# VectorE's complex products in fewer, longer operations: a third plane with minus the imaginary part, and products over both parts at once

## The chip, the cores and the metric

The kernel runs on one core of one Trainium2 chip. The metric is the device time of one execution in microseconds (us). The engines are named as in the profile: PE is TensorE, DVE is VectorE, ACT is ScalarE, POOL is GpSimd, SP is SyncE, which issues most of the DMAs. Each engine works through its own queue in order; they wait for each other at semaphores.

## What is computed

A linear attention with a complex decay, then a mixture of four experts over its output:

```python
B, H, S, D = 4, 8, 768, 48
a_n = a * min(|a|, 0.999) / (|a| + 1e-6)        # complex, a = a_re + i a_im
for t in range(S):                              # state S_t: complex, D x D for each batch and head
    state = a_n[t][:, None] * state + outer(k[t], v[t])
    y[t]  = q[t] @ real(state)
x = y as [B*S, H*D]                             # 3072 x 384
out = sum over e of p[:, e] * (relu(x @ w1[e]) @ w2[e])     # 4 experts, F = 1024, p normalised over e
```

All is float32.

## The kernel before

**Groups and chunks.** The 3072 rows are cut into 12 groups of 256 steps (g), three for each batch, and a group into two chunks of 128. A tile with q, k or a of a group has 128 partitions (head and feature) and 8 x 96 columns for each part: 8 steps in a row (SEG, index i) times 96 segments (MS: 3 blocks of heads by 32).

**From a to Q and K, on VectorE and ScalarE.** `load_a` (L355) brings the real and the imaginary part of a into a tile A of two buffers. `norm` (L399) finds the factor and multiplies A by it in place (L438). `prefix` (L441) turns A into running products: for i = 1 to 7 one product of all four combinations (L446), a subtract (L448) and an add (L449); then over the segments of a chunk with doubling width (`sk`, through `cmul`, L383: products L387 and L388, subtract L394, add L395); then the fill of all other steps (`fm`, products L390 to L393 one part at a time, then L394 and L395). `finish` (L483) has a head (L508), which finds the squared magnitude with a reduction that keeps the least value for a check at the end (L513, into `st_a2`), and multiplies q by A (L520), and a tail (L531), which divides k by A (L535 to L543). `rotate` (L685) multiplies the state by the product of a whole group: two products across the halves (L694, L695), one in place (L696), a sum (L697).

**What sets the order.** For group 0 all this stands alone at the start (`front(0, ...)`, L888): TensorE only splits the first weights, runs dummy matmuls (`turn_over`, L217) and does the small products of the near attention. From there `moe1(g - 1)` runs the experts 0 and 1 of one group on TensorE (`ph` L246 and `po` L267, each with float32 split in a high and a low part: `xh`/`xl`, `hh`/`hl`), and `between` (L942) weaves the front and the attention of the next groups in, by costs written out by hand (the numbers behind `yield`, STEP and MORE). In 4 steps of `moe1` an expert is done; its copies go to `acc` (L775) and by a POOL DMA to memory. The order on each engine is then fixed by a planner that goes by modelled lengths. The groups 0 and 1 use the near form, in two halves for the two chunks; the later ones do both chunks at once. At about 580 us the second stage begins (`c2`, L971): experts 2 and 3 in a form with fewer products (L995), in tiles that take the place of the first stage's.

Of the kernel before, what the change touches and what calls it, by code (L numbers as in the profile page):

```python
# [8 lines left out]
F32 = mybir.dt.float32  # L9
# [22 lines left out]
NA = 2  # L32
# [21 lines left out]
PRE = ("acc", "xh", "xl")  # L54
# [71 lines left out]
def fast_path(ctx, tc, qkP, aP, vP, probsP, w, out, flag):  # L126
# [54 lines left out]
    def stage1(i, tags):  # L181
        return stage_w(i, 1, moe.tile([P, 2 * HD], F32, tag=tags[i % len(tags)], name=f"wst{i}",
                                        bufs=1 if tags[i % len(tags)] == "x" else None))[:, 0]
# [114 lines left out]
    with ExitStack() as c1:  # L298
# [19 lines left out]
        nc.scalar.activation(maskp, m_ps[:, :2], AF.Copy)  # L318
# [8 lines left out]
        st_a2 = big.tile([P, CG, NG], F32, name="st_a2")  # L327
# [11 lines left out]
        nc.gpsimd.memset(TA, 0.0)  # L339
        band = moe.tile([P, HOFF + P + IM + C], F32, tag="x", name="band", bufs=1)  # L340
# [3 lines left out]
        nc.scalar.activation(near_mask, m_ps[:, 2], AF.Copy)  # L344
# [28 lines left out]
        def cmul(x, br, bi, shape, nm):  # L373
# [24 lines left out]

        def norm(g, A, parts=((0, SEG),), prev=(None, None, None)):  # L399
            s = tmp(f"s{g}")  # L400
            u = tmp(f"u{g}")
            for n, (lo, hi) in enumerate(parts):
# [35 lines left out]
                nc.vector.tensor_tensor(Af, Af, bc2(y0), op=ALU.mult)  # L438
                yield 1.75

        def prefix(g, A, cuts=(1, NS)):  # L441
            for i in range(1, SEG):
# [40 lines left out]
        def finish(g, A, qk):  # L483
# [24 lines left out]
            def head(lo, hi):  # L508
                nc.scalar.activation(some(a2a, lo, hi), some(A[:, 0], lo, hi), AF.Square)
                nc.scalar.activation(some(b2a, lo, hi), some(A[:, 1], lo, hi), AF.Square)  # L510
                for c in range(lo, hi):
                    a2, ic = some(a2a, c, c + 1), some(i0a, c, c + 1)
                    red = nc.vector.tensor_tensor_reduce(a2, a2, some(b2a, c, c + 1), scale=1.0, scalar=3e38,  # L513
                                                         op0=ALU.add, op1=ALU.min, accum_out=st_a2[:, c, g:g + 1])
# [4 lines left out]
                for c in range(2):  # L519
                    ins = nc.vector.tensor_tensor(dst(Q[:, c, :, :C], lo, hi), rows(A[:, c], lo, hi),  # L520
                                                  rows(qk[:, 0], lo, hi), op=ALU.mult)
                    if g < NSEL and lo == 1:
                        behind(ins, red)
                        last["qp"] = ins
# [6 lines left out]
            def tail(lo, hi):  # L531
# [5 lines left out]
                nc.vector.tensor_tensor(t, kn, t, op=ALU.mult)  # L537
                for c in range(2):
                    to, x, y = dst(K[0][:, c], lo, hi), rows(A[:, c], lo, hi), rows(ta, lo, hi)
                    if hi - lo == CG:  # L540
                        to = K[0][:, c].rearrange("p n (f i s) -> p (n f) i s", f=2, i=SEG)
                        x, y = (z.rearrange("p i (n s) -> p n i s", s=CS // 2) for z in (A[:, c], ta))
                    last_dve = nc.vector.tensor_tensor(to, x, y, op=ALU.mult)  # L543
# [15 lines left out]
        def t_factors(g):  # L559
# [5 lines left out]
            tc.keep_in_program_order(nc.scalar.activation(TB[IM:M], Ti, AF.Copy))  # L565
            tc.keep_in_program_order(nc.scalar.activation(TB[0:D], Ti, AF.Copy, scale=-1.0))
# [118 lines left out]
        def rotate(g):  # L685
# [96 lines left out]
        def check_all():  # L782
            nc.vector.tensor_scalar(st_m2, st_m2, M2_MIN, None, op0=ALU.is_ge)
            for c in range(CG):
                nc.vector.tensor_scalar(st_a2[:, c], st_a2[:, c], A2_MIN[c], None, op0=ALU.is_ge)
            nc.vector.tensor_scalar(st_w, st_w, W_MAX, None, op0=ALU.is_le)
            for c in range(CG):
                nc.vector.tensor_tensor(st_m2[:, :NG], st_m2[:, :NG], st_a2[:, c], op=ALU.mult)
# [10 lines left out]

# [744 lines left out]
```

## Time and profile before

| | |
|---|---|
| median of 3 runs | 961.46 us (960.48 to 963.05) |
| the profiled execution | 960.0 us, its span 958.2 us |
| granted TensorE clock | 0.999 of full speed |
| busy: PE, DVE, ACT, POOL | 933.9, 745.2, 483.0, 210.7 us |
| instructions: PE, DVE, ACT, POOL | 7388, 1630, 1030, 294 |
| chain that ended last | PE 89%, DVE 6%, DMA 3%, ACT 2% |

The span goes from the first to the last instruction; the rest of the execution's time lies around it. A row of the timeline gives the start, the length, engine, line, operation, output and inputs with their shapes; brackets at its end give the idle time before it and what ended that. In the table of stretches each engine has its busy time and the number of its instructions. A row of waits gives who waited for whom, the total in us, how often, and the longest.

### The profile page before, as it was taken

What the parts mean: (1) busy time and instruction counts of PE and PEld (TensorE: products, weight loads), DVE (VectorE), ACT (ScalarE), POOL (GpSimd) and SP (SyncE); (2) the same over time, 40 slices, a digit from 0 to 9 for tenths busy, and PEclk for the clock granted to TensorE, in tenths of its full rate; (3) what the DMA queues carried; (4) which work ended last, traced back from release to release, by engine and by line L of the source; (5) the groups of instructions that cost most, each with busy time, mean ns of one, the idle gap of its engine ahead of it and who ended that gap; (6) DMA issues with size and microseconds to landing.
All of it is one profiled execution on the core that took longest, in us unless ns stands there. A gap on an engine that the chain in (4) does not pass through costs nothing.

```text
span 958.2 us, 19409 instructions
## 1 busy us (share of the span) xinstructions
PE 933.9 (97%) x7388; PEld 908.3 (95%) x7388; DVE 745.2 (78%) x1630; ACT 483.0 (50%) x1030; POOL 210.7 (22%) x294
## 2 busy tenths in 40 slices
PE   5999999999999999999999999999999999999997
PEld 3899999999999999999999999999999999999997
DVE  7898989989989999888996577748485757666642
ACT  7766446363564736547343555635454554444430
POOL 6030111020211202111111036333424352322000
PEclk9999999999999999999999999999999999999999
DMA  9585264544535546353437799131514433131112
GB/s 314 171 172 139 60 159 89 150 99 142 149 96 129 129 138 156 117 135 109 117 109 226 269 316 275 50 121 38 148 57 144 162 85 102 50 99 51 50 50 78
DMA packets 75029, 125.73 MB, mean 131 GB/s; under 512 B 9600, under 2 KB 50224, under 8 KB 74928
## 3 DMA queue, kind: packets, MB, share of 16 engines
q1 hardware_dynamic: 60464, 94.69, 32.7%
q0 software_dynamic: 14464, 29.72, 13.3%
q8 instruction: 60, 0.98, 0.5%
q14 instruction: 41, 0.34, 0.1%
HBM read 75.94 MB, written 31.46 MB: 112 GB/s over the span
## 4 chain that ended last, share of the span: by engine, by line
PE 89%; DVE 6%; DMA 3%; ACT 2%; issue 1%; SPq 0%; ACTq 0%; DVEq 0%
PE ph L246 21%; PE pob L995 20%; PE po L267 19%; PE pb L995 17%; PE sc L635 3%; PE yp L667 2%; PE dp L611 2%; PE yp L677 2%; PE ktp L584 1%; DMA RX<-w 1%; PE sc L652 1%; DMA shi<-late_d 1%; DVE pf L446 1%; PE xp L706 1%; DVE xl L1001 0%
## 5 line engine op out<-in xcount | busy, mean ns | idle before, releaser
L995 PE MATMUL pob<-shi,hid 128*128 128x384 f32 x528 | 148.5, 335 | 0.5 <-DVE hid L1004 0.5
L267 PE MATMUL po<-whi,hh 128*128 128x384 f32 x384 | 129.7, 338 | 0.0
L267 PE MATMUL po<-wlo,hh 128*128 128x384 f32 x384 | 128.9, 336 | 0.0
L257 ACT ACTIVATE hh<-ph 128x512 fp32r<-128x512 f32 x96 | 57.2, 596 | 121.8 <-PE ph L246 117.5
L1007 POOL TENSOR_TENSOR Z<-Z 128x384 f32<-128x384 f32 x84 | 89.9, 1104 | 114.6 <-DMA Z<-y_d 57.0
L246 PE MATMUL ph<-xha,whi 128*128 128x256 f32 x576 | 103.8, 287 | 1.3 <-ACT xha L233 1.3
L246 PE MATMUL ph<-xla,whi 128*128 128x256 f32 x576 | 101.0, 283 | 2.0 <-DVE xla L235 2.0
L246 PE MATMUL ph<-xha,wlo 128*128 128x256 f32 x576 | 102.0, 284 | 0.0
L995 PE MATMUL pb<-xh,shi 128*128 128x384 f32 x291 | 97.1, 335 | 1.0 <-DVE pb L1001 1.0
L995 PEld LDWEIGHTS pob<-shi,hid 128*128 128x128 f32 x528 | 96.4, 188 | 1.2 <-DVE hid L1004 1.1
L995 PE MATMUL pb<-xl,shi 128*128 128x384 f32 x288 | 96.2, 334 | 0.0
L995 PE MATMUL pb<-xh,slo 128*128 128x384 f32 x288 | 96.2, 334 | 0.0
L246 PEld LDWEIGHTS ph<-xha,whi 128*128 128x128 f32 x576 | 85.9, 190 | 5.3 <-issue 2.4
L258 DVE SCALAR_TENSOR_TENSOR hl<-ph,hh 128x512 fp32r<-128x512 f32 x96 | 65.9, 687 | 31.0 <-ACT hh L257 30.3
L995 PE MATMUL pob<-slo,hid 128*128 128x384 f32 x264 | 88.2, 334 | 0.0
L267 PE MATMUL po<-whi,hl 128*128 128x384 f32 x384 | 85.2, 338 | 0.5 <-DVE hl L258 0.5
L246 PEld LDWEIGHTS ph<-xla,whi 128*128 128x128 f32 x576 | 82.8, 191 | 2.7 <-DVE xla L235 2.4
L246 PEld LDWEIGHTS ph<-xha,wlo 128*128 128x128 f32 x576 | 82.8, 190 | 0.4
L998 ACT ACTIVATE SN<-pb 128x384 f32<-128x384 f32 x96 | 47.4, 494 | 66.7 <-PE pb L995 59.4
L1001 DVE TENSOR_TENSOR xl<-Z,xh 128x384 fp32r<-128x384 f32 x104 | 59.2, 598 | 21.7 <-ACT xh L998 16.3
L998 ACT ACTIVATE hid<-pb 128x384 fp32r<-128x384 f32 x76 | 37.3, 491 | 71.9 <-PE pb L995 71.5
L267 PEld LDWEIGHTS po<-whi,hh 128*128 128x128 f32 x384 | 72.4, 189 | 0.3 <-ACT acc L775 0.2
(238 smaller groups left out, 2119.4 us busy)
## 6 DMA issues: line engine op xcount, KB each, us to landing
qk<-qkP SPq DMA_DIRECT2D x24, 384.0 KB, 4.0
acc_d<-acc POOLq DMA_DIRECT2D x24, 384.0 KB, 5.3
ACC<-acc_d SPq DMA_DIRECT2D x48, 192.0 KB, 3.2
A<-aP SPq DMA_DIRECT2D x22, 384.0 KB, 6.1
v<-vP SPq DMA_DIRECT2D x24, 288.0 KB, 3.0
Z<-y_d SPq DMA_DIRECT2D x16, 384.0 KB, 4.8
Qst<-Q SPq DMA_DIRECT2D x40, 145.1 KB, 3.9
Kst<-K SPq DMA_DIRECT2D x40, 144.0 KB, 3.8
```

Source lines behind the costliest of these rows:

```text
L246: ins = nc.tensor.matmul(ph[:, u, :], wt[:, j * P:(j + 1) * P], xt[:, j, :], start=(n == 0), stop=(n == 3 * NJ - 1))
L257: wts["hh"] = nc.scalar.activation(hh, ph, AF.Relu)
L258: nc.vector.scalar_tensor_tensor(hl, ph, 0.0, hh, op0=ALU.max, op1=ALU.subtract)
L267: nc.tensor.matmul(po[t], part[0][:, u, t * P:(t + 1) * P], wts[i][n][:, HD:], start=(i % FE == 0 and part[0] is hh and n == 0), stop=(i % ...
L611: ins = nc.tensor.matmul(d_ps[o:o + n, h, :], KT[:, c, h, o:o + n], vc[:, h * D:(h + 1) * D], start=True, stop=True)
L635: ins = nc.tensor.matmul(to, k, q, start=True, stop=True)
L667: ins = nc.tensor.matmul(yo, vc[:, vo:vo + n], scs[2 * c + h // 4][:, h % 4, :], start=True, stop=first)
L677: ins = nc.tensor.matmul(yo, st[:, o:o + n], Qc[:, o // D, :], start=False, stop=True)
L995: return tc.keep_in_program_order(nc.tensor.matmul(*args, **kw))
L998: return pin(nc.scalar.activation(dst, src, fn, scale=scale))
L1001: pin(nc.vector.tensor_tensor(dst, x, y, op=op))
L1007: nc.gpsimd.tensor_tensor(dst, x, y, op=op)
```

## The change

The normalised a goes to a new tile N with three planes: minus the imaginary part, the real part, the imaginary part. VectorE writes planes 1 and 2 from A; ScalarE writes plane 0 as a negated copy of plane 2, in two pieces. With it a prefix step is one product and one sum over both parts in place of a product, a subtract and an add; the first step of the later groups keeps the old form. The first level of the scan has one product in place of two, the fill has two products over both parts in place of four, and for the groups from 2 on Q and K have one product each in place of two. The reduction of the head becomes a plain add; the value for the check is copied out by ScalarE. In `rotate` ScalarE copies the state's halves across, and one product over all partitions follows. A and N have one buffer each, where A had two, so that the load of the next a comes behind the normalisation; `acc` goes from two buffers to one, one staged weight goes to the tile `y`, and one hidden tile of the second stage to another pool. The masks' copies on ScalarE come behind the negation.

```diff
@@ PRE and stage1
-PRE = ("acc", "xh", "xl")
+PRE = ("acc", "xh", "xl", "y", "xh", "xl")
...
+        tag = tags[i % len(tags)]
+        pool = small if tag == "y" else moe
...
@@ constants of the first stage
-        nc.scalar.activation(maskp, m_ps[:, :2], AF.Copy)
-        st_a2 = big.tile([P, CG, NG], F32, name="st_a2")
+        st_a2 = big.tile([P, NG, NJ, CG], F32, name="st_a2")
...
+        nc.gpsimd.memset(TB, 0.0)
...
-        nc.scalar.activation(near_mask, m_ps[:, 2], AF.Copy)
@@ load_a
-            A = big.tile([P, 2, SEG, MS], F32, tag="A", name=f"A{g}", bufs=NA)
+            A = big.tile([P, 2, SEG, MS], F32, tag="A", name=f"A{g}", bufs=1)
@@ cmul
-            if len(shape) < 3:
-                nc.vector.tensor_tensor(v1, x, bc2(br), op=ALU.mult)
-                nc.vector.tensor_tensor(v2, x, bc2(bi), op=ALU.mult)
+            if shape[1:] == [1]:
+                z = tmp(f"{nm}z").rearrange("p c n -> p (c n)")[:, :4 * n].rearrange("p (c d n) -> p c d n", c=2, d=2)
+                v1, v2 = (z[:, k].unsqueeze(3) for k in range(2))
+                part, (col, _), _ = br.ap
+                nc.vector.tensor_tensor(z, x[:, :, :, 0].unsqueeze(1).broadcast_to([P, 2, 2, n]),
+                                        bass.AP(br.tensor, br.offset, [part, (SEG * MS, 2), (0, 2), (col, n)]), op=ALU.mult)
             else:
-                nc.vector.tensor_tensor(v1[:, 0], x[:, 0], br, op=ALU.mult)
-                nc.vector.tensor_tensor(v2[:, 1], x[:, 1], bi, op=ALU.mult)
-                nc.vector.tensor_tensor(v1[:, 1], x[:, 1], br, op=ALU.mult)
-                nc.vector.tensor_tensor(v2[:, 0], x[:, 0], bi, op=ALU.mult)
+                nc.vector.tensor_tensor(v1, x, both(br), op=ALU.mult)
+                nc.vector.tensor_tensor(v2, x, both(bi), op=ALU.mult)
@@ norm
+            N = planes[g] = big.tile([P, 3, SEG, MS], F32, tag="N", name=f"N{g}", bufs=1)
...
-                nc.vector.tensor_tensor(Af, Af, bc2(y0), op=ALU.mult)
+                last["an"] = nc.vector.tensor_tensor(N[:, 1:, lo:hi].rearrange("p c i m -> p c (i m)"), Af, bc2(y0),
+                                                     op=ALU.mult)
+                rows = (max(lo, 1), hi) if hi - lo < SEG else (2, 5, SEG)
+                for r0, r1 in zip(rows, rows[1:]):
+                    last["neg"] = nc.scalar.activation(N[:, 0, r0:r1], N[:, 2, r0:r1], AF.Copy, scale=-1.0)
@@ prefix
-                nc.vector.tensor_tensor(z, x.unsqueeze(2).broadcast_to([P, 2, 2, MS]), bc2(A[:, :, i - 1, :]),
-                                        op=ALU.mult)
-                nc.vector.tensor_tensor(x[:, 0], z[:, 0, 0], z[:, 1, 1], op=ALU.subtract)
-                nc.vector.tensor_tensor(x[:, 1], z[:, 1, 0], z[:, 0, 1], op=ALU.add)
+                if g > 0 and i == 1:
...
+                else:
+                    w, b = N[:, :2, i, :], N[:, 2, i - 1, :]
+                    part, plane, col = w.ap
+                    nc.vector.tensor_tensor(z, bass.AP(w.tensor, w.offset, [part, plane, plane, col]),
+                                            bass.AP(b.tensor, b.offset, [part, (-plane[0], 2), (0, 2), col]),
+                                            op=ALU.mult)
+                    nc.vector.tensor_tensor(x, z[:, 0], z[:, 1], op=ALU.add)
@@ finish, head and tail
+                red = nc.vector.tensor_tensor(some(a2a, lo, hi), some(a2a, lo, hi), some(b2a, lo, hi), op=ALU.add)
                 for c in range(lo, hi):
                     a2, ic = some(a2a, c, c + 1), some(i0a, c, c + 1)
-                    red = nc.vector.tensor_tensor_reduce(a2, a2, some(b2a, c, c + 1), scale=1.0, scalar=3e38,
-                                                         op0=ALU.add, op1=ALU.min, accum_out=st_a2[:, c, g:g + 1])
...
+                if hi - lo == CG:
+                    nc.vector.tensor_tensor(Q[:, :, :, :C].rearrange("p c n (i s) -> p i c n s", i=SEG),
...
+                ends = a2a.rearrange("p i (j n s) -> p j n i s", j=NJ, n=CG)[:, :, lo:hi, SEG - 1, CS - 1]
+                behind(nc.scalar.activation(st_a2[:, g, :, lo:hi], ends, AF.Copy), last_act)
...
@@ rotate (t_factors writes TB with the signs exchanged)
-            nc.vector.tensor_tensor(turned[0:D], Gt[IM:M], bt(TB[IM:M]), op=ALU.mult)
-            nc.vector.tensor_tensor(turned[IM:M], Gt[0:D], bt(TB[0:D]), op=ALU.mult)
+            nc.scalar.activation(turned[0:D], Gt[IM:M], AF.Copy)
+            nc.scalar.activation(turned[IM:M], Gt[0:D], AF.Copy)
             nc.vector.tensor_tensor(Gt, Gt, bt(TA), op=ALU.mult)
+            nc.vector.tensor_tensor(turned, turned, bt(TB), op=ALU.mult)
@@ moe1, late_weights, grab
-                acc = moe.tile([P, CG, HD], F32, tag="acc", name=f"acc{g}_{e}")
+                acc = moe.tile([P, CG, HD], F32, tag="acc", name=f"acc{g}_{e}", bufs=1)
-            raw = big.tile([P, 4, NJ, P], F32, tag="A", name=f"lw{i}", bufs=NA)
+            raw = big.tile([P, 4, NJ, P], F32, tag="AN"[len(late_raw) % 2], name=f"lw{i}", bufs=1)
-                    tag = {0: "x", 1: "xh", 2: "xl", 7: "xh", 8: "xl", 9: "acc", 10: "acc"}[k]
+                    tag = {0: "x", 1: "xh", 2: "xl", 7: "xh", 8: "xl", 9: "acc", 10: "hid"}[k]
...
@@ the start
-        A.append(load_a(1))
         for _ in norm(0, A[0], parts=halves):
             pass
+        A.append(load_a(1, prev=last["an"]))
         lin = last["lin"]
+        behind(nc.scalar.activation(maskp, m_ps[:, :2], AF.Copy), last["neg"])
+        behind(nc.scalar.activation(near_mask, m_ps[:, 2], AF.Copy), last["neg"])
...
-            lp = split_w(i, wst[i], ((ps_o, "po"), (ps_h, "ph")), prev=lin)
+            lp = split_w(i, wst[i], ((ps_o, "po"), (ps_h, "ph")), prev=lin if i < NPRE - 1 else last["neg"])
```

## Rows read from the trace of the kernel before

**Rows 1.** The page, part 1: busy time, share of the span, instructions.

```profile
PE 933.9 (97%) x7388; PEld 908.3 (95%) x7388; DVE 745.2 (78%) x1630; ACT 483.0 (50%) x1030; POOL 210.7 (22%) x294
```

**Rows 2.** Table of stretches: length, busy time by engine, clock, DMA share, GB/s.

```profile
25.00:50.00 25.00, 23.27 (x238) 20.52 (x237) 20.38 (x44) 18.15 (x40) 1.95 (x4) 1.00 0.51 158
...
150.00:200.00 50.00, 47.34 (x449) 45.03 (x449) 46.28 (x100) 26.24 (x55) 5.91 (x12) 1.00 0.42 108
200.00:500.00 300.00, 299.98 (x2952) 291.70 (x2951) 275.25 (x621) 153.93 (x326) 39.05 (x73) 1.00 0.49 128
...
550.00:610.00 60.00, 58.48 (x371) 57.15 (x370) 41.57 (x87) 35.10 (x77) 28.66 (x35) 1.00 0.87 246
...
950.00:958.20 8.20, 1.95 (x12) 1.63 (x10) 0.62 (x1) 0.00 (x0) 0.00 (x0) 0.94 0.11 32
```

**Rows 3.** Waits of TensorE, whole span: us in total, times, longest.

```profile
PE ph L246 <- DVE xla L235: 2.0, 1, 2.0
PE ph L246 <- ACT xha L233: 1.3, 2, 0.7
...
PE ktp L584 <- DVE K L543: 0.6, 1, 0.6
...
PE qp L478 <- DVE Q L520: 0.2, 1, 0.2
```

**Rows 4.** Timeline of VectorE at the start: start, length, line, operation.

```profile
15.72 0.56 DVE L446 TENSOR_TENSOR pf<-A 128x384 f32<-128x384 f32 x1
16.31 0.26 DVE L448 TENSOR_TENSOR A<-pf 128x96 f32<-128x96 f32 x1
16.49 0.25 DVE L449 TENSOR_TENSOR A<-pf 128x96 f32<-128x96 f32 x1
16.77 0.56 DVE L446 TENSOR_TENSOR pf<-A 128x384 f32<-128x384 f32 x1
...
20.00 0.26 DVE L387 TENSOR_TENSOR sk_1a<-A 128x96 f32<-128x96 f32 x1
...
20.47 0.21 DVE L394 TENSOR_TENSOR A<-sk_1a 128x48 f32<-128x48 f32 x1
...
23.18 0.48 DVE L390 TENSOR_TENSOR fm_1a<-A 128x315 f32<-128x315 f32 x1
...
24.89 0.48 DVE L394 TENSOR_TENSOR A<-fm_1a 128x315 f32<-128x315 f32 x1
```

**Rows 5.** Timeline at the stall near 150 us, VectorE and TensorE.

```profile
149.34 0.83 DVE L390 TENSOR_TENSOR fm_1a<-A 128x651 f32<-128x651 f32 x1
...
152.33 0.55 DVE L235 TENSOR_TENSOR xla<-xp,xha 128x384 fp32r<-128x384 f32 x1
...
152.93 0.62 PE L246 MATMUL ph<-xla,whi 128*128 128x256 f32 x3 [1.99 <-DVE xla L235]
```

**Rows 6.** Timeline behind the first normalisation, VectorE and ScalarE.

```profile
9.21 0.96 DVE L438 TENSOR_TENSOR A<-A,u 128x768 f32<-128x768 f32 x1
...
9.90 0.52 ACT L427 ACTIVATE u<-u 128x384 f32<-128x384 f32 x1
10.20 0.57 DVE L446 TENSOR_TENSOR pf<-A 128x384 f32<-128x384 f32 x1
...
14.50 0.60 ACT L435 ACTIVATE u<-u,neg 128x384 f32<-128x384 f32 x1
```

**Rows 7.** ScalarE's groups by line, up to 560 us: busy us, mean ns | idle before.

```profile
L588 ACT ACTIVATE KT<-ktp 128x288 f32<-128x288 f32 x40 | 16.7, 417 | 26.3 <-PE ktp L584 26.3
...
L619 ACT ACTIVATE Gs<-dp 112x384 f32<-112x384 f32 x4 | 2.0, 492 | 12.8 <-PE dp L611 12.8
```

**Rows 8.** Timeline: first reader of the second a, first matmul of the experts.

```profile
35.84 0.85 ACT L407 ACTIVATE s<-A 128x768 f32<-128x768 f32 x1
...
50.56 0.62 PE L246 MATMUL ph<-xha,whi 128*128 128x256 f32 x3 [0.58 <-ACT xha L233]
```

**Rows 9.** Waits of ScalarE from 60 to 550 us.

```profile
ACT hh L257 <- PE ph L246: 114.5, 53, 6.6
```

More of the change, by code (lines that the diff above doesn't have):

```diff
@@ L31 @@
 TMP = 4
-NA = 2
 NF1 = E1 * FE
@@ L181, in stage1 @@
     def stage1(i, tags):
-        return stage_w(i, 1, moe.tile([P, 2 * HD], F32, tag=tags[i % len(tags)], name=f"wst{i}",
-                                        bufs=1 if tags[i % len(tags)] == "x" else None))[:, 0]
+        tag = tags[i % len(tags)]
+        pool = small if tag == "y" else moe
+        return stage_w(i, 1, pool.tile([P, 2 * HD], F32, tag=tag, name=f"wst{i}",
+                                       bufs=1 if tag in ("x", "y", "acc") else None))[:, 0]
     def cast_w(i):
@@ L518, in head @@
                     last_act = nc.scalar.activation(ic, ic, AF.Exp, scale=-1.0, bias=a2e[:, c:c + 1])
[L519 to L524, printed above, removed]
+                if hi - lo == CG:
+                    nc.vector.tensor_tensor(Q[:, :, :, :C].rearrange("p c n (i s) -> p i c n s", i=SEG),
+                                            A.rearrange("p c i (n s) -> p i c n s", n=NR),
+                                            rows(qk[:, 0], lo, hi).unsqueeze(2).broadcast_to([P, SEG, 2, NR, CS]),
+                                            op=ALU.mult)
+                else:
+                    for c in range(2):
+                        ins = nc.vector.tensor_tensor(dst(Q[:, c, :, :C], lo, hi), rows(A[:, c], lo, hi),
+                                                      rows(qk[:, 0], lo, hi), op=ALU.mult)
+                        if lo == 1:
+                            behind(ins, red)
+                            last["qp"] = ins
+                ends = a2a.rearrange("p i (j n s) -> p j n i s", j=NJ, n=CG)[:, :, lo:hi, SEG - 1, CS - 1]
+                behind(nc.scalar.activation(st_a2[:, g, :, lo:hi], ends, AF.Copy), last_act)
                 if hi == CG:
@@ L784, in check_all @@
             for c in range(CG):
-                nc.vector.tensor_scalar(st_a2[:, c], st_a2[:, c], A2_MIN[c], None, op0=ALU.is_ge)
+                nc.vector.tensor_scalar(st_a2[:, :, :, c], st_a2[:, :, :, c], A2_MIN[c], None, op0=ALU.is_ge)
             nc.vector.tensor_scalar(st_w, st_w, W_MAX, None, op0=ALU.is_le)
             for c in range(CG):
-                nc.vector.tensor_tensor(st_m2[:, :NG], st_m2[:, :NG], st_a2[:, c], op=ALU.mult)
+                for j in range(NJ):
+                    nc.vector.tensor_tensor(st_m2[:, :NG], st_m2[:, :NG], st_a2[:, :, j, c], op=ALU.mult)
             nc.vector.tensor_tensor(st_m2, st_m2, st_w, op=ALU.mult)
@@ L830, in fast_path, with front @@
         qk = load_qk(0)
-        A.append(load_a(1))
         for _ in norm(0, A[0], parts=halves):
             pass
+        A.append(load_a(1, prev=last["an"]))
         lin = last["lin"]
+        behind(nc.scalar.activation(maskp, m_ps[:, :2], AF.Copy), last["neg"])
+        behind(nc.scalar.activation(near_mask, m_ps[:, 2], AF.Copy), last["neg"])
         cuts = (1, NS // CG, NS)
         todo = {}
-        def front(g, A, qk):
-            pre = prefix(g, A, cuts if g < NSEL else (1, NS))
-            Q, K, head, tail = finish(g, A, qk)
+        def front(g, qk):
+            pre = prefix(g, cuts if g < NSEL else (1, NS))
+            Q, K, head, tail = finish(g, planes[g][:, 1:], qk)
             def ahead():
@@ L885, in fast_path @@
         for i in range(NPRE):
-            lp = split_w(i, wst[i], ((ps_o, "po"), (ps_h, "ph")), prev=lin)
+            lp = split_w(i, wst[i], ((ps_o, "po"), (ps_h, "ph")), prev=lin if i < NPRE - 1 else last["neg"])
         turn_over(WARM[0], lp)
-        for _ in front(0, A[0], qk):
+        for _ in front(0, qk):
             pass
@@ L907, in stream @@
                     A.append(load_a(g + 1, prev=last["q"]))
-                for r in front(g, A[g], qk):
+                for r in front(g, qk):
                     yield g, r
@@ L1186, in grab @@
                 else:
-                    tag = {0: "x", 1: "xh", 2: "xl", 7: "xh", 8: "xl", 9: "acc", 10: "acc"}[k]
-                    t = moe.tile([P, 2 * TB2], F32R, tag=tag, name=f"hid{k}", bufs=1 if tag == "x" else None)
+                    tag = {0: "x", 1: "xh", 2: "xl", 7: "xh", 8: "xl", 9: "acc", 10: "hid"}[k]
+                    t = (fin if tag == "hid" else moe).tile([P, 2 * TB2], F32R, tag=tag, name=f"hid{k}",
+                                                            bufs=1 if tag in ("x", "acc", "hid") else None)
                 return t[:, :TB2], t[:, TB2:]
```

33 lines of the change are left out of this document (25 added, 8 removed).

## The prediction

> **What bounds the kernel now.** I read the engine shares first. TensorE is busy 97% of the span, VectorE 78%, ScalarE 50% [rows 1]. A change of VectorE's work can therefore only win back time in which TensorE stands still, and the share of 78% says nothing yet. The second view is the table of stretches [rows 2]; in it the reader is to compare TensorE's busy time with the length of each stretch. From 200 to 500 us it is busy 299.98 of 300 us although VectorE is busy 275.25 of them: there, less work on VectorE buys nothing. TensorE's idle time lies in four places: the start (25 to 50 us is 1.7 us idle, though much of its work there is dummy matmuls of `turn_over`, which hold nothing up), 2.7 us in 150 to 200, 1.5 us in 550 to 610, and 6.2 us behind 950, where the last rows are only written out. The third view, TensorE's waits [rows 3], says which of it is VectorE's: 2.0 us at one place for `xla` (L235), 0.6 us for K (L543), 0.2 us for Q (L520). The waits for `xha` (1.3 us) end on ScalarE and DMA, and VectorE has no part in them.
>
> So two places decide. **The start:** from the first normalised half to the first K, VectorE runs one chain of dependent operations: the prefix over 8 rows, the scan, the fill [rows 4]. **One stall at 150 us:** TensorE waits for the second `xla` piece of group 2, which stands in VectorE's queue behind four fill products, and starts 0.6 us after it [rows 5].
>
> **The price of a VectorE operation.** An operation of 96 elements lasts 0.25 us and the next one that does not need its result starts 0.18 us after it; one that needs it starts 0.28 us after it [rows 4]. One of 651 elements lasts 0.83 us, and four in a row take 2.99 us, 0.75 each [rows 5]. Hence 1.045 ns for an element (0.58 us over 555), some 0.15 us fixed in the duration, but only 0.07 us fixed between starts. From that, as estimates: 192 elements 0.35 us, 630 elements 0.81, 1302 elements 1.51. A merge of two independent operations saves 0.07 us, not 0.15.
>
> **The start, added up.** A prefix step now goes subtract, add, next product: 0.46 us from L448 to the next L446 [rows 4]. With one sum of 192 elements it is 0.35 + 0.03 = 0.38: 0.08 saved, in seven steps 0.56. The first scan level has two products in 0.47 us up to L394 [rows 4]; as one of 192 elements 0.38: 0.09 saved. The fill has four products in 1.71 us up to its subtract [rows 4]; as two of 630 elements 0.73 + 0.81 + 0.03 = 1.57: 0.14 saved, and the second fill of group 0 lies on the same chain: 0.28. The reduce of the head loses its accumulator read, but its result goes to ScalarE at the same moment: 0. Together 0.93 us.
>
> Against it stands a new hop. The prefix of group 0 needs the negated plane from its first step, so after the normalisation (L438 at 9.21, 0.96 long) ScalarE has to negate rows 1 to 3 before the first product, which now starts at 10.20 [rows 6]. ScalarE is in L427 until 10.42; the negation, 288 elements, costs 0.42 by the nearest row [rows 7]; so the product could start at 10.86, 0.66 late. If VectorE puts L428, which needs only L427, ahead of it, 0.28 us are lost instead. The second half's negation may stand behind L435 (14.50, 0.60 long and a read [rows 6]); that gives 0 to 0.4 us at step 4. The small copy of `st_a2` stands on ScalarE ahead of the K transposes' eviction: 0.1. The hop costs 0.3 to 1.1 us; I take 0.5, nearer the low end, because the other half's normalisation is there to fill it. Net gain 0.4 us; bounds 0.65 gained and 0.2 lost. TensorE sets a lid as well: in front of Q and K it only waits 0.2 + 0.6 us [rows 3], the rest is dummy matmuls in its queue, so no more than 0.8 us can be won before the first K.
>
> **The stall at 150 us.** Since VectorE's last idle moment before it (a wait for scores) its queue holds six pairs of subtract and add, the first scan level and the four fill products. 6 x 0.08 + 0.09 + (2.99 - 2 x 1.43 = 0.13) = 0.70 us. If the order stays, `xla` comes 0.7 us earlier and the stall falls from 2.0 to 1.3. But the program's order is computed anew from the changed lengths, and where `xla` lands among two longer products is open: between all 2.0 us won and 0.8 lost (one product of 1.51 us started just before it in place of one of 0.75). I take 0.7.
>
> **What is hidden.** In each later group VectorE loses about 1.4 us: six steps 0.48, scan 0.09, fill 0.13, head 0.1, Q and K 0.07 each, and of `rotate` one operation of 384 elements, 0.55 by the same price (eight times in all). ScalarE gains two negations of 0.42, two copies of 0.49 in `rotate` [rows 7] and a small one: about 2.0 us a group, at 50% use. TensorE does not wait for VectorE from 200 to 500 [rows 2], so both count 0 while that cover holds.
>
> **New waits, and who stands behind them.** (1) The product of row 2 waits for ScalarE's negation; behind it on VectorE stand `hl` (L258) and `xla`, and TensorE waits for those. (2) `rotate`'s copies wait on ScalarE for VectorE's increment; behind them stand `hh` and `xha`. The turned state is needed by the next group only; its cover is TensorE's MoE work of a whole group. (3) A has one buffer, so its load waits for the normalisation. For A1 that means a start near L435's 14.50 [rows 6] instead of ahead of it, with the v loads behind; its reader is L407 at 35.84 [rows 8], 20 us later: 0. The later loads may hold SP, with v loads, y stores and sends behind; v is wanted a good part of a group later: 0. (4) `acc` has one buffer: the second expert's copies (L775) wait until POOL's transfer of the first has read it, with four MoE steps between: 0. (5) The staged weight in `y`, `hid` in another pool, the extra clear on POOL: 0, but the new layout may move what the last stage's loads wait for. There TensorE idles 1.5 us of 60 [rows 2]; I take 0, and from 1.0 gained to 3 lost.
>
> **The sum.** The profiled execution took 960.0 us: 958.2 of span and 1.8 around it. 960.0 - 0.4 - 0.7 = 958.9. The median of the runs shown is 961.46, 1.5 above the profiled one, so in its terms 960.4. That is 0.1%; about 0.3% (2.9 us) is what a measurement of this kernel can tell from no change.
>
> **Rivals.** *A, the whole stall goes:* the new order puts `xla` ahead of the fill, and the start reaches its lid. 0.8 + 2.0: 958.7. For it: the piece was ready on ScalarE's side before the fill began. Against: nothing in the change aims at that order. 0.15.
> *B, nothing is left:* the hop eats the start's gain and the stall stays: 961.5. For it: the hop's upper bound is above the saving. 0.17.
> *C, a merged operation saves its whole fixed part,* 0.15 us: the start would save 7 x 0.15 + 0.15 + 4 x 0.15 = 1.8, and stop at the lid of 0.8; the stall falls by 6 x 0.15 + 0.15 + 0.3 = 1.35. Together 2.15: 959.3. Against it: L449 starts 0.18 us after L448, which lasts 0.26 [rows 4]. 0.05. [...]
> *D, slower: ScalarE hands the negation over late.* ScalarE works in order and stands 53 times in front of `hh` for TensorE, 114.5 us in all, 2.2 us at a time, at most 6.6 [rows 9]. Where the negation is queued behind such a wait, VectorE stands at row 2 with `hl` and `xla` behind it. One step (L446 at 15.72 to the next at 16.77, 1.05 us [rows 4]) covers it; 1.1 us a group are left, in ten groups 11, and with half of it reaching TensorE 5.5: 967. It decides once VectorE's spare time in a group is used up: 24.7 us idle in 300 [rows 2], about 3.5 a group (some seven groups lie there), plus the 1.4 saved. That is why I give it only 0.12.
> *E, the change does not do all it says:* single buffers and the new layout delay the last stage's loads by about 3 us: 964.5. 0.06.
>
> **How the numbers follow.** The forecast has 0.45, with its own range 959.0 to 961.6. Faster by over 0.3% (under 958.6): half of A, and the lower tails of the forecast and C: 0.12. Slower (over 964.3): D and half of E: 0.15. Within: 0.73. The range from 957.4 to 964.3 takes in A with the spread of the runs, B, C and the lower half of E, and leaves out D.
>
> **What would show it.** Right: L448 and L449 become one operation of about 0.35 us and a step of 0.97; the first `ph` starts 0.2 to 0.8 us before its 50.56 [rows 8]; the wait for `xla` near 150 us shrinks to about 1.3; TensorE stays full from 200 to 500. Wrong: waits of VectorE for the negation of more than 0.5 us, TensorE idle behind `hl`, or later loads at 550 us.

## The result and the profile after

| | kernel before | changed kernel |
|---|---|---|
| median of 5 runs each, us | 961.46 (960.48 to 963.05) | 968.43 (966.77 to 968.71) |
| ratio to before, 95% interval | | 1.0067 (1.0052 to 1.0081) |
| profiled execution, us (span) | 960.0 (958.2) | 968.48 (966.8) |

The change makes the kernel 7 us slower, 0.67%. The prediction, 960.4 us and no difference that can be measured, was wrong, and the time lies above its range.

The page's first part for the changed kernel, to be held against [rows 1]:

```profile
span 966.8 us, 19282 instructions
## 1 busy us (share of the span) xinstructions
PE 936.0 (97%) x7388; PEld 910.2 (94%) x7388; DVE 733.5 (76%) x1459; ACT 500.0 (52%) x1084; POOL 210.5 (22%) x295
```

VectorE does what the change says: 171 instructions and 11.7 us less. ScalarE has 54 instructions and 17 us more. TensorE's own work has hardly grown (936.0 against 933.9 us), so three quarters of the loss (6.5 of 8.6 us of span) is TensorE standing still. Its waits over the whole span (us in total, times, longest), against [rows 3]:

```profile
PE po L268 <- ACT acc L810: 3.8, 2, 1.9
PE ph L247 <- ACT xha L234: 2.2, 1, 2.2
PE ph L247 <- DVE hl L259: 1.9, 2, 1.0
PE po L268 <- ACT hh L258: 1.8, 2, 1.0
PE qp L503 <- DVE Q L550: 1.8, 1, 1.8
```

The stall of 2.0 us for `xla` [rows 3, 5], which the prediction expected to shrink, is gone. In its place stand waits for ScalarE that were not there, for `acc` and `hh`, a longer one for `xha`, and two for `hl` on VectorE; the wait for Q lies at the start, before the experts. The table of stretches says where (columns as in [rows 2]):

```profile
200.00:500.00 300.00, 295.27 (x2911) 286.40 (x2910) 266.27 (x516) 159.94 (x350) 39.30 (x74) 1.00 0.49 127
550.00:610.00 60.00, 57.14 (x363) 56.34 (x362) 39.60 (x85) 30.55 (x65) 22.84 (x29) 0.97 0.95 279
```

From 200 to 500 us TensorE now idles 4.7 us where it idled 0.02 [rows 2], and that with VectorE 9 us less busy. To see where the time goes I follow one instruction through all kernels: the same `ph` matmul starts so much later (+) or earlier (-) than in the kernel before, in us. In a kernel whose TensorE works in another order, a lag also holds work that stands elsewhere: in the changed kernel it is -1.9 us at 441 us and +6.8 at 449. So I go by differences that stay, and by the waits beside them.

| starts before at | 50.6 | 149.3 | 194.9 | 326.6 | 457.9 | 502.4 | 545.4 | 578.3 |
|---|---|---|---|---|---|---|---|---|
| changed kernel | +1.9 | +1.2 | -0.6 | -0.2 | +5.1 | +5.6 | +5.5 | +8.0 |
| e1_rot | +1.9 | +4.4 | +2.5 | +2.6 | +6.9 | +6.9 | +6.3 | +5.5 |
| e2_neg1 | +0.3 | +0.6 | +1.3 | +3.0 | +9.9 | +10.3 | +10.3 | +11.0 |
| e4_noneg | -0.1 | +0.6 | +3.0 | +4.5 | +7.0 | +7.8 | +8.6 | +9.1 |
| e3_lay | 0.0 | 0.0 | 0.0 | -0.3 | -0.3 | -0.3 | -0.3 | -0.1 |
| f1_fill | -0.3 | +0.2 | -0.1 | +1.1 | +2.0 | +1.6 | +2.5 | +3.0 |
| g1_fillo | -0.3 | -0.4 | -0.5 | -0.7 | -0.7 | -0.8 | -0.8 | -0.9 |
| g2_fqho | -0.2 | -0.2 | +1.1 | +1.3 | +1.3 | +8.3 | +8.2 | +8.3 |
| g3_layo | 0.0 | +0.6 | +1.9 | +3.3 | +4.4 | +4.0 | +4.9 | +5.4 |
| g4_allo | -0.2 | +0.9 | 0.0 | +1.3 | +2.8 | +8.4 | +8.4 | +8.0 |
| h1_fqh | -0.2 | -0.2 | -0.2 | +0.2 | +0.3 | +0.3 | +0.3 | +0.2 |
| h2_all | -0.2 | +0.9 | +0.4 | +1.2 | +2.3 | +3.5 | +3.4 | +3.5 |
| h3_xla | -0.2 | -0.2 | +1.3 | +1.7 | +1.8 | +1.8 | +1.7 | +1.4 |
| h4_nego | 0.0 | +2.3 | +1.7 | +1.4 | +1.4 | +1.4 | +1.4 | +1.3 |
| h5_layaft | +1.0 | +2.4 | +0.7 | +0.9 | +6.6 | +7.0 | +7.0 | +9.4 |
| h7_best | -0.2 | -0.2 | -1.1 | -0.7 | -0.5 | -0.5 | -0.5 | -0.7 |

The changed kernel loses in three places: at the start, between 326 and 458 us, and at the change to the second stage. **The start**, VectorE's and ScalarE's timeline, beside [rows 4] and [rows 6]:

```profile
10.84 2.29 ACT L199 ACTIVATE whi<-wst 128x768 fp32r<-128x768 f32 x3
13.04 0.43 ACT L453 ACTIVATE N<-N 128x288 f32<-128x288 f32 x1
...
13.50 0.56 DVE L471 TENSOR_TENSOR pf<-N 128x384 f32<-128x384 f32 x1
14.09 0.36 DVE L474 TENSOR_TENSOR N<-pf 128x192 f32<-128x192 f32 x1
14.48 0.56 DVE L471 TENSOR_TENSOR pf<-N 128x384 f32<-128x384 f32 x1
...
32.62 1.02 DVE L576 TENSOR_TENSOR K<-N,u 128x384 f32<-128x384 f32 x2
```

The pairs have become one operation of 0.36 us and the step takes 0.98 us instead of 1.05, but the first product starts at 13.50 instead of 10.20: the negation (L453) stands behind three weight casts on ScalarE. K comes at 32.62 instead of 32.45. Then, at group 1's normalisation, ScalarE and TensorE:

```profile
48.95 0.18 ACT L446 ACTIVATION_READ_ACCUMULATOR u<-u,neg 128x1 f32 x1
50.89 0.78 ACT L453 ACTIVATE N<-N 128x288 f32<-128x288 f32 x2 [1.76 <-DVE N L449]
51.57 0.85 ACT L234 ACTIVATE xha<-xp 128x384 fp32r<-128x384 f32 x2
...
52.48 0.62 PE L247 MATMUL ph<-xha,whi 128*128 128x256 f32 x3 [2.23 <-ACT xha L234]
```

ScalarE stands for 1.76 us at the negations until VectorE has written N, with `xha` behind them, and the experts begin at 52.48 instead of 50.56 [rows 8].

**The groups.** The longest wait among them, at 452 us, ScalarE and TensorE:

```profile
448.94 0.51 ACT L728 ACTIVATE Gs<-Gs 48x384 f32<-48x384 f32 x1
449.46 0.52 ACT L729 ACTIVATE Gs<-Gs 48x384 f32<-48x384 f32 x1
450.00 0.60 ACT L258 ACTIVATE hh<-ph 128x512 fp32r<-128x512 f32 x1
450.50 0.93 ACT L429 ACTIVATE s<-s,m2b 128x768 f32<-128x768 f32 x1
451.32 1.04 ACT L810 ACTIVATE acc<-po,pr 128x384 f32<-128x384 f32 x2
...
451.95 0.44 PE L268 MATMUL po<-whi,hh 128*128 128x384 f32 x1 [1.89 <-ACT acc L810]
```

The turn's two copies and a step of the next normalisation stand ahead of the copy of `acc` out of `po`, and TensorE waits 1.89 us for that copy before its next `po`. Taken over the 53 or 54 `hh` between 200 and 500 us, one starts 0.90 us after the last matmul of its `ph` on average, before 0.52 us.

**The second stage.** ScalarE, TensorE and the stretches around it:

```profile
572.30 1.77 ACT L1039 ACTIVATE xh<-Z 128x384 fp32r<-128x384 f32 x4 [5.66 <-DMA Z<-y_d]
...
575.68 1.03 ACT L810 ACTIVATE acc<-po,pr 128x384 f32<-128x384 f32 x2
...
576.29 0.44 PE L268 MATMUL po<-whi,hh 128*128 128x384 f32 x1 [1.88 <-ACT acc L810]
...
576.70:580.00 3.30, 3.30 (x12) 3.30 (x11) 3.30 (x9) 2.16 (x7) 1.44 (x2) 0.50 0.67 190
```

ScalarE waits 5.66 us for Z, whose casts are queued ahead of `acc`; TensorE stands for 1.88 us and then runs at half its clock (0.50) for some 3.4 us, which costs about 1.7 us more (an estimate, half of the 3.4 us).

### The profile page after: what moved, and what is told of

It reads as the page before. It is cut to its first block, busy times and chain, and to the rows that moved or that the text cites. A ratio compares the mean times of both kernels' runs of the same rounds, so it can differ in the third digit from the quotient of the medians.

```text
span 966.8 us, 19282 instructions
## 1 busy us (share of the span) xinstructions
PE 936.0 (97%) x7388; PEld 910.2 (94%) x7388; DVE 733.5 (76%) x1459; ACT 500.0 (52%) x1084; POOL 210.5 (22%) x295
## 4 chain that ended last, share of the span: by engine, by line
PE 78%; DVE 10%; ACT 6%; DMA 4%; issue 2%; SPq 0%; ACTq 0%; DVEq 0%
PE pob L1036 20%; PE po L268 17%; PE ph L247 16%; PE pb L1036 16%; PE sc L669 3%; PE dp L645 1%; PE ktp L618 1%; PE yp L701 1%; DMA Z<-y_d 1%; DVE scs L680 1%; PE yp L711 1%; PE sc L686 1%; DVE N L402 1%; DMA late_d<-lwl 1%; DVE pf L471 1%
```

## The experiments

No kernel leaves out part of the computation. A ratio is to runs of the kernel before on the same chip, with its 95% interval.

### Undoing one part of the change

**e1_rot** puts the turn back on VectorE (and the signs of `t_factors` with it):

```diff
-            nc.scalar.activation(turned[0:D], Gt[IM:M], AF.Copy)
-            nc.scalar.activation(turned[IM:M], Gt[0:D], AF.Copy)
+            nc.vector.tensor_tensor(turned[0:D], Gt[IM:M], bt(TB[IM:M]), op=ALU.mult)
+            nc.vector.tensor_tensor(turned[IM:M], Gt[0:D], bt(TB[0:D]), op=ALU.mult)
             nc.vector.tensor_tensor(Gt, Gt, bt(TA), op=ALU.mult)
-            nc.vector.tensor_tensor(turned, turned, bt(TB), op=ALU.mult)
```

> The changed kernel with the state's turn put back on VectorE (two products of 48 rows from Gs and TB, no ScalarE copies); all else as changed. Theory S (three separate causes: the copies of the turn stand on ScalarE ahead of hh and acc in the groups after 320; the negations delay the first product; the new layout delays the last stage's loads): TensorE's lag on the kernel before stays +1.9 us at the first ph, falls from +5.6 to about +1 at 502 us, and the time to about 964 us. Rival L (one buffer for A and acc is behind the waits of the groups): 968 us, the waits between 326 and 458 stay. Rival M (VectorE, with fewer operations, takes the next group's norm ahead of hl): 968 us, and the waits on hl stay while those on acc and hh go.

Measured: 965.71 us, 1.0057 (1.0044 to 1.0071). 2.7 us better, but the lag at 502 us is +6.9, not +1, and new waits on `hl` and `acc` of 1.3 to 1.5 us appear at 114, 364 and 409 us. The gain lies at the second stage, where the wait for `acc` at 576 us is gone: the lag at 578 us is +5.5 instead of +8.0.

**e2_neg1** issues group 1's negations behind `xha` of group 0:

```diff
-                for r0, r1 in zip(rows, rows[1:]):
+                for r0, r1 in zip(rows, rows[1:]) if g != 1 else ():
...
         x[0] = split_x(0, x[0])
+        for r0, r1 in ((2, 5), (5, SEG)):
+            N1 = planes[1]
+            behind(nc.scalar.activation(N1[:, 0, r0:r1], N1[:, 2, r0:r1], AF.Copy, scale=-1.0), wts["x"])
```

> The changed kernel with one thing moved: group 1's two negations are issued on ScalarE behind xha of group 0 instead of ahead of it. Theory S: xha starts at about 49.0 us and the first ph at 50.8 us instead of 52.5, 1.7 us earlier, and, if no later wait takes it back, the time is about 966.7 us. Rival (the stall at 150 us, which the late start had swallowed, comes back: the lag was -0.6 at 195 us after all): first ph 50.8 us, but the lag at 200 us is again what the changed kernel has, 968.4 us.

Measured: 971.49 us, 1.0113 (1.0098 to 1.0129). The first `ph` starts at 50.82 as expected, and the kernel is 3 us *slower* than the changed one: +9.9 us at 458. Neither theory has this. Moving two instructions at 51 us had changed what happens 400 us later.

**e4_noneg** has no negated plane and the prefix of the kernel before in all groups, and keeps the rest:

```diff
-                for r0, r1 in zip(rows, rows[1:]):
-                    last["neg"] = nc.scalar.activation(N[:, 0, r0:r1], N[:, 2, r0:r1], AF.Copy, scale=-1.0)
...
-                    nc.vector.tensor_tensor(x, z[:, 0], z[:, 1], op=ALU.add)
+                nc.vector.tensor_tensor(x[:, 0], z[:, 0, 0], z[:, 1, 1], op=ALU.subtract)
+                nc.vector.tensor_tensor(x[:, 1], z[:, 1, 0], z[:, 0, 1], op=ALU.add)
```

> The changed kernel without any negated plane: the prefix is that of the kernel before (product, difference, sum) in all groups, nothing else is put back (fills, Q, K, the turn's copies as changed). Theory S: first ph back at about 50.4 us (2 us earlier); the copies' waits after 320 us stay; 966.5 us. Rival A (ScalarE is simply too full, each group's two negations of 0.4 to 0.5 us are as guilty as the two copies of 0.5 us): lag at 502 us falls to about +2 too, 963 us. Rival V (VectorE's 6 more operations a group cost as much as ScalarE gains): 968 us.

Measured: 968.77 us, 1.0080 (1.0067 to 1.0094). First `ph` at 50.45, and all of it lost again by 195 us. Theory S, three separate causes, does not explain these three: each cure works at its place and something else opens elsewhere.

### The layout alone

**e3_lay** has the buffers, loads and issue rules of the changed kernel with all operations of the kernel before. Against the kernel before only lines of this kind differ:

```diff
-            A = big.tile([P, 2, SEG, MS], F32, tag="A", name=f"A{g}", bufs=NA)
+            A = big.tile([P, 2, SEG, MS], F32, tag="A", name=f"A{g}", bufs=1)
...
+            N = planes[g] = big.tile([P, 3, SEG, MS], F32, tag="N", name=f"N{g}", bufs=1)
...
-                acc = moe.tile([P, CG, HD], F32, tag="acc", name=f"acc{g}_{e}")
+                acc = moe.tile([P, CG, HD], F32, tag="acc", name=f"acc{g}_{e}", bufs=1)
```

> The buffers, loads and issue order of the changed kernel (A one buffer, N of three planes, acc one buffer, the staging tags, the last hid in fin, late raw weights in A and N), with all operations of the kernel before on VectorE and ScalarE: no negation, prefix in three operations, four products of the fills, two each of Q and K, the turn on VectorE. Theory S: only the transition to the second stage is late (the second pair of Z's loads waits, about 2.5 us with the half clock behind it): lag about 0 until 545 us, 964 us in all. Rival L (the buffers make the groups' waits too): lag already +4 at 500 us, 967 us or more. Rival N (the layout costs nothing by itself): 961.5 us.

Measured: 961.17 us, 1.0009 (1.0000 to 1.0018): the layout costs nothing, at the second stage neither (-0.1 at 578). Rival N was right; theory S falls here too, and L with it. This kernel is the base of what follows, because its order of instructions on ScalarE, VectorE and TensorE is exactly that of the kernel before.

### One part alone, on that base

Each kernel is e3_lay with one hunk of the change's diff: **f1_fill** that of `cmul`, **f2_qk** the merged Q and K, **f3_head** the sum over both chunks with the copy of the ends, **f4_turn** that of `rotate` and `t_factors`.

> The new buffers with the old operations (e3_lay, 961.2 us) and one part of the change: the fills' products over both parts at once (630, 672 and 1302 elements instead of two each of half) and sk_1's product in one. Theory W (what costs is the work put on ScalarE; the merged VectorE operations themselves are harmless): 960.5 us, no more than 0.5 us over or 1 us under e3_lay. Rival O (any part that makes VectorE's chain shorter brings ScalarE's background work, squares, logarithms and exponentials, into other places ahead of hh, and costs 2 us or more by itself): 963 us or more, with new waits on hh or acc between 200 and 500 us.

> e3_lay and one part: Q and K for both parts in one operation of 1536 elements (about 1.75 us instead of two of 0.96 us). Theory W: 961 us. Rival O: 963 us or more, waits on hh or hl in the groups. Rival B (a long operation stands ahead of hl and lets it wait up to 0.8 us longer): waits on hl, not on hh, 962 to 963 us.

> e3_lay and one part: the sum of the squares over both chunks in one operation, with the ends copied by ScalarE (one copy of 0.2 us a group). Theory W: 961.2 us, at most +0.5 us for 12 short copies. Rival O: 963 us or more, since both logarithms and both exponentials now come ready together and stand as one stretch of 2.2 us ahead of hh.

> e3_lay and one part: the turn of the state with two copies on ScalarE of 0.5 us each and two products on VectorE. Theory W: 963 to 965 us, with waits on hh and acc after 320 us as in the changed kernel (putting the turn back in the changed kernel gave 2.7 us). Rival O: the same as any other part, 963 us. Rival N (the copies cost only in company with the others): 961.2 us.

| | us | ratio | in the base's order: ScalarE (of 1017), TensorE (of 6291) |
|---|---|---|---|
| f1_fill | 965.73 | 1.0051 (1.0037 to 1.0065) | 933, 6034 |
| f2_qk | 962.72 | 1.0021 (1.0012 to 1.0030) | 969, 6082 |
| f3_head | 964.84 | 1.0045 (1.0031 to 1.0058) | 954, 6060 |
| f4_turn | 964.88 | 1.0041 (1.0027 to 1.0055) | 947, 6084 |
| changed kernel | 968.43 | 1.0067 (1.0052 to 1.0081) | 876, 5925 |

Each part by itself costs 1.5 to 4.5 us, the fills the most, though they put nothing on ScalarE. Theory W falls with f1_fill, f2_qk and f3_head. O stands in the main: f2_qk is 0.3 us under its 963 us and in the range of rival B, but B's waits on `hl` are not in its trace; the new ones are on `xha` (1.88 us at 198 us) and `hh` (0.95 at 204). The parts don't add up either: over e3_lay the four make 13.5 us, the whole change 7.3. The last column points at what they have in common. It counts, over the longest sequence that both have, how many of the base's instructions keep their order. The planner, which goes by modelled lengths, gave every one of these kernels another order, also on TensorE, where no instruction is different.

### The order held

The order of a kernel can be imposed on another one: a table of places is written into the kernel, and each instruction gets an order-only edge to the one that shall stand ahead of it. A merged operation stands where the last of its pair stood. This was done for ScalarE, VectorE, TensorE and SyncE; GpSimd's queue was left to the planner, and the program's own order rules were dropped where the table contradicts them.

```python
        order = [k for a, n in runs for k in range(a, a + n)]
        for a, b in zip(order, order[1:]):
            tc.add_manual_dep(mine[b], mine[a].name,
                              mybir.DependencyInfo(mybir.DependencyClass.NoSync, mybir.DependencyReason.DATA),
                              reason="issue order")
```

> f1_fill (965.7 us: the fills' products over both parts, nothing else of the change's operations) with the issue order of all engines but GpSimd held to that of e3_lay (961.2 us), a merged product standing where the last of its pair stood; left to itself the planner that orders the program puts some 80 of ScalarE's 1017 instructions and 260 of TensorE's 6291 elsewhere. Theory Q (what a part of the change costs is the other order that the planner gives the queues, not the operation): 960.5 to 961.5 us, and no new waits on hh or acc. Rival B (the longer operations themselves hold up what stands behind them): 965 us, as f1_fill.

> The mirror of g1_fillo: the operations of e3_lay, all of the kernel before, in the issue order that the planner gave f1_fill. Theory Q: about 965 us, though no operation differs from e3_lay's. Rival B: 961 us.

**g1_fillo**: 961.10 us, 1.0002 (0.9993 to 1.0011). **g3_layo**: 967.17 us, 1.0059 (1.0045 to 1.0072). The pair settles the fills: the new operations in the old order cost nothing, the old operations in the new order cost 6 us. TensorE's waits from 45 to 610 us, f1_fill first, then g1_fillo, then g3_layo:

```profile
PE ph L247 <- DVE xla L236: 2.6, 2, 1.8
PE po L268 <- ACT acc L788: 2.2, 2, 1.2
```

```profile
PE ph L380 <- DVE xla L369: 1.8, 1, 1.8
PE po L401 <- ACT hh L391: 0.5, 1, 0.5
```

```profile
PE ph L384 <- DVE xla L373: 2.9, 2, 2.0
PE po L405 <- ACT acc L917: 2.3, 2, 1.2
```

The two waits on `acc` go with the order, not with the operations.

> Three parts of the change (fills, Q and K, the sum of squares with its copies on ScalarE) in e3_lay's issue order; each alone, planned freely, cost 1.5 to 4.5 us. Theory Q: 960 to 961.5 us, a little under the kernel before at best, since the saved work of VectorE lies beside TensorE. Rival B: the sum of the three, some 970 us, or at least 965 us.

> All operations of the changed kernel in e3_lay's issue order; the negations and the turn's copies stand on ScalarE at the place that the trace of e3_lay gives for the moment when their input is ready, so group 1's negations come behind xha. Theory Q: 961 to 962.5 us (0.5 us may stay for VectorE's waits on the negations and for 40 more operations on ScalarE). Rival W (the added work on ScalarE costs by itself): 964 us or more, with hh late again. Rival B: 968 us as the changed kernel.

**g2_fqho**: 967.84 us, 1.0070 (1.0056 to 1.0085). **g4_allo**: 968.49 us, 1.0080 (1.0065 to 1.0095). Both miss theory Q. Most of it is one place between 458 and 502 us, where the lag grows by 7.0 and 5.6 us; g2_fqho, ScalarE and VectorE:

```profile
492.26 0.20 ACT L676 ACTIVATE st_a<-s 128x6 f32<-128x6 f32 x1
...
492.49 0.19 DVE L939 TENSOR_SCALAR st_a<-st_a 128x36 f32<-128x36 f32 x1 [4.18 <-ACT st_a L676]
```

In the old order the check of the states stands on VectorE right behind the sum that fed it. With the change ScalarE's copy feeds it, for which VectorE waits 4.18 us with `hl` queued behind; TensorE then stands 3.96 us for `hl` at 498.60 in g2_fqho, and some 3 us more go by a granted clock of 0.50 from 498 to 504 us (an estimate, half of the 6 us). An order is only good for the dependences it was made for. h1_fqh and h2_all move these ten operations to where the check's last one stands:

```diff
-VectorE: sum of squares; check of st_a2, st_m2; Q; ...; hl; ...; good<-cut,good
+VectorE: sum of squares; Q; ...; hl; ...; check of st_a2, st_m2; good<-cut,good
```

> g2_fqho (fills, Q and K, sum of squares, in e3_lay's issue order) with the ten operations of the check at the end of the state's part moved some 16 us later on VectorE, ahead of the last of them. Theory Q (order): the wait of 4.2 us on ScalarE's copy and the 7 us at 460 to 500 us go: 960.5 to 962.5 us (the half clock behind the stall at 150 us, 1.7 us, may stay). Rival B (the longer operations cost by themselves): 964 us or more.

> g4_allo (all operations of the change in e3_lay's issue order) with the check's operations moved in the same way. Theory Q: 962 to 963.5 us: the lag was +1.5 us from 240 to 410 us and +3.0 at 458 us, which is what the negations and copies cost in a good place. Rival W (the work put on ScalarE is the larger part): the lag at 580 us stays over +4 us, 965 us or more.

> The operations of the kernel before with the buffers of the changed one (e3_lay, 961.2 us), in the issue order that the planner gave the changed kernel. Theory Q: 965 to 968 us, though none of the change's operations is in it. Rival W: below 963 us, since no negation and no copy is there.

**h1_fqh**: 961.19 us, 1.0006 (0.9997 to 1.0015). Three parts that alone cost 4.5, 1.5 and 3.7 us cost nothing together. **h2_all**: 964.91 us, 1.0045 (1.0032 to 1.0059); it falls between the theories: the order gives back a third of the 7 us by the ratios, half by the medians. **h5_layaft**: 970.69 us, 1.0095 (1.0081 to 1.0109): the old operations in the changed kernel's order are slower than the changed kernel itself. Its waits of TensorE from 45 to 610 us, with no negation and no copy of the turn in it:

```profile
PE ph L385 <- DVE hl L397: 3.2, 2, 2.2
PE po L406 <- ACT acc L918: 2.9, 2, 1.9
```

They lie at 363 and 408 us (`hl`) and at 453 and 578 us (`acc`), the places where the changed kernel stands. At 453 us the wait is 0.98 us, not 1.89, so the copies had a share there; at 578 us it is the same 1.89. How much of h5_layaft's time comes of an order that was made for other dependences, as in g2_fqho, is open.

The lag of h2_all grows in three steps. At 93 us a negation stands between two copies of KT, and TensorE waits 1.76 us for KT, in h1_fqh 0.68. At 450 us it waits 0.72 us for `hl`, which stands on VectorE behind the turn's products, and these behind work that ScalarE does after the turn's copies. The third step is at 495 us, ScalarE and TensorE:

```profile
492.87 0.52 ACT L864 ACTIVATE Gs<-Gs 48x384 f32<-48x384 f32 x1
493.40 0.52 ACT L865 ACTIVATE Gs<-Gs 48x384 f32<-48x384 f32 x1
...
495.19 0.44 PE L404 MATMUL po<-whi,hh 128*128 128x384 f32 x1 [1.16 <-ACT acc L946]
```

The turn's copies take 1.04 us of ScalarE ahead of `acc`, and TensorE waits 1.16.

> e3_lay (old operations, new buffers, 961.2 us) with the negations and the two-operation prefix alone, in e3_lay's issue order, each negation on ScalarE at the moment when its input is ready. Theory Q: 961 to 962.5 us; the wait for KT near 92 us, where a negation of 0.8 us stands between two copies of KT, is some 1 us longer as in h2_all, and the rest hides. Rival W (12 groups of 0.8 us more on ScalarE): 964 us.

**h4_nego**: 961.27 us, 1.0001 (0.9992 to 1.0010). The negations alone cost nothing in a good order, so of the 3.7 us between h1_fqh and h2_all the copies, or both together, have most; the copies stand in two of the three steps above. The copies alone in a held order were not tried.

### Can the saved time be had?

h1_fqh with one and then two more changes of the order:

```diff
 h3_xla
-VectorE: sums of sk_16; fm_1a; fm_1b; xla of group 2, second half
+VectorE: sums of sk_16; xla of group 2, second half; fm_1a; fm_1b
 h7_best, beside that
-ScalarE: squares of group 3; hh of group 2
+ScalarE: hh of group 2; squares of group 3
-VectorE: sum of squares of group 3; hl of group 2
+VectorE: hl of group 2; sum of squares of group 3
```

> h1_fqh with one instruction more moved: the second half of xla of group 2, which TensorE awaits at 152.9 us, stands on VectorE ahead of the fills of group 3 instead of behind their products. Theory Q: the stall of 2.0 us goes and nothing behind it can take it back, since the order is held: 959 us, under both kernels. Rival: a later wait (xha at 195 us, hl) takes it back: 961 us.

> h3_xla with two instructions more moved, so that the gain of 2.0 us is not passed on: the first hh of group 2 stands on ScalarE ahead of the squares of group 3, its hl on VectorE ahead of their sum. Theory Q: TensorE's wait of 1.9 us on hh and the half clock behind it go, lag at 300 us about -1.5 us against e3_lay, 959 to 959.5 us, under both kernels. Rival (each stall taken out is given back at the next wait, xha at 195 us): 961 us.

**h3_xla**: 961.96 us, 1.0011 (1.0002 to 1.0020). **h7_best**: 960.81 us, 1.0002 (0.9993 to 1.0011). Neither beats the kernel before. TensorE in h3_xla, then in h7_best:

```profile
155.47 0.61 PE L404 MATMUL po<-whi,hh 128*128 128x384 f32 x1 [1.90 <-ACT hh L394]
```

```profile
171.58 0.40 PE L793 MATMUL sc<-Qst,Kst 112*64 112x128 f32 x2 [1.48 <-DMA Kst<-K]
```

With `xla` early the 2.0 us turn up 3 us later as a wait for `hh`, which stands behind squares that wait for the fills. With `hh` early too they turn up 19 us later, 1.48 of them, as a wait for K's DMA. The attention's chain through ScalarE, VectorE and DMA is hardly earlier: K's product starts at 163.9 us against 164.2 in h1_fqh, the scores at 171.6 against 172.1. The stall at 150 us was only the place where TensorE met that chain first.

## Why the prediction was wrong

**What held.** The price of an operation: 192 elements 0.36 us (0.35 forecast), a prefix step 0.98 (0.97), two fill products of 630 elements 1.58 us from the first to the subtract (1.57). Rival C's 0.15 us a merge did not come: a step gained 0.07 (1.05 us before, 0.98 now), the fixed share between two starts that the forecast had worked out from [rows 4]. One buffer for A and `acc`, and the layout: costed at 0, and e3_lay's 1.0009 bears it out. Rival E's place was hit in the changed kernel, not its cause: the layout alone is on time there, the old operations in the new order are not (h5_layaft, +7.0 to +9.4).

**The step that failed: "What is hidden".** It counted VectorE's saving and ScalarE's 2.0 us a group as 0 "while that cover holds", because TensorE did not wait from 200 to 500 us. But the cover was an order: each `hh`, `hl` and `acc` stood in its queue so that it came in time. The prediction did say that the order is computed anew, and drew it into the sum at one place only, for `xla` at 150 us. It holds for every place: 141 of 1017 instructions on ScalarE and 366 of 6291 on TensorE stand elsewhere in the changed kernel. g1_fillo, g3_layo, h1_fqh and h5_layaft show that this alone makes 0 or 6 to 10 us of the same operations. In the changed kernel, going back to the old order is worth 2 to 3.5 us of the 7 (h2_all, by the ratios and by the medians). Some 4 us stay, and they go with ScalarE's added work, the other term that was counted as 0. Why the planner's other orders come out worse on the chip was not tried; its modelled lengths are the obvious suspect, no more.

**The new waits.** (2), the turn's copies, were costed at 0 by looking at who reads the turned state. `hh` and `xha` were named as standing behind them, and that should have been the price: at most two copies of 0.5 us, eight times, 8 us. h2_all against h1_fqh gives 3.7 us, which the copies share with the negations. (1) was looked at from one side: rival D let VectorE wait for the negation. At 49 us it is ScalarE that waits 1.76 us for VectorE with `xha` behind it, a term of the sum that was missing. D's 967 us is near the result by chance: its own sign, VectorE waiting over 0.5 us for a negation, is nowhere in the trace. Another sign of being wrong did come, TensorE idle behind `hl`, 0.90 us at 361 us and 1.03 at 406, behind operations that wait 2.27 and 2.24 us for ScalarE's squares.

**The start.** The hop was sized at 0.3 to 1.1 us; the first product came 3.3 us later, since the weight casts had got ahead of the negation. VectorE filled the time with the other half, as forecast, so K lost 0.17 us where 0.4 were to be gained.

**The stall at 150 us.** Forecast 1.3 us, it went to 0, as in rival A, but not for A's reason. The second half of `xla` still stands behind both fill products; in the new order the first of these starts at 145.54 us instead of 149.34:

```profile
145.54 1.51 DVE L400 TENSOR_TENSOR fm_1a<-N 128x1302 f32<-128x1302 f32 x1
...
149.46 0.55 DVE L236 TENSOR_TENSOR xla<-xp,xha 128x384 fp32r<-128x384 f32 x1
```

What it gave did not last: TensorE waits 1.01 us for `hh` at 156.63, and the lag, +1.2 us at 149 and -0.6 at 195, is back at +0.7 at 239. h3_xla and h7_best show why it could not have given 2 us.

## What to carry to other kernels

Where a planner fixes the order from modelled lengths, a changed operation is two changes, and the second one can be the larger: compare the orders of the two programs before anything else, and hold the old order to see what the operation itself costs. Work moved to an engine at 50% use is not free if what the bound engine waits for stands behind it in the same queue (3.7 us between h1_fqh and h2_all); price it by its neighbours, not by who reads its result. And a stall taken out is a gain only if the chain that ends there is itself shorter, otherwise it turns up again at the next meeting point (in h3_xla 1.90 of 2.0 us, 3 us later).

## What was not expected of the hardware

A short stop of TensorE cost about as much again in some of the profiled executions: stretches of 3.4 us at a granted clock of 0.50 follow stops of 1.38 us (h4_nego, at 93 us), 1.88 (changed kernel, 576 us) and 1.90 us (h3_xla, 155 us), each costing about 1.7 us, by the estimate above. In h4_nego the lag shows it: it goes from 0.0 to +2.3 us by 149 us with only 0.7 us more of waiting. The same stop did not always do so: behind 2.0 us of waiting the kernel before stays at 1.00, and g2_fqho drops to 0.50 behind a stop of 1.81 us at 152.5 us where h1_fqh, with the same stop of 1.81 us at 152.51, does not. Over all twenty traces, 11 of the 35 stops of 1.3 to 2.3 us between 50 and 945 us are followed by such a stretch. The stretches behind it, the kernel before, then g2_fqho, then h1_fqh:

```profile
152.90:156.00 3.10, 3.07 (x25) 3.07 (x26) 2.19 (x5) 2.08 (x3) 0.00 (x0) 1.00 0.53 94
```

```profile
153.40:156.60 3.20, 3.20 (x16) 3.20 (x16) 2.29 (x4) 2.02 (x3) 0.00 (x0) 0.50 0.26 51
```

```profile
153.40:156.60 3.20, 3.20 (x26) 3.20 (x26) 2.29 (x4) 2.76 (x5) 0.00 (x0) 1.00 0.32 63
```

So lags of 1.7 us between two of these profiles can be the clock and not the program; the verdicts above rest on the medians.
